# A threshold-attention and MLP kernel: mask operations split around the threshold, rounded weights used a step later, one plain MLP chunk, and no making up of MLP work that had to wait

## The chip, the cores and the metric

The kernel runs on one core of one Trainium2 chip. A core has five engines with a queue each: TensorE (PE in the profile; PEld is its weight loading), VectorE (DVE), ScalarE (ACT), GpSimd (POOL) and SyncE (SP), which here only issues transfers. PE writes into PSUM banks; the other engines move and change data in SBUF and PSUM. Each queue is worked off in order, and an instruction waits until what it reads is written and what it overwrites has been read. The metric is the time of one execution in microseconds (us), and the median of several executions is compared.

## The reference

Eight batches of eight heads, 576 positions, head width 64. Attention keeps only the scores that come within `tau` of the row's maximum; the result, 4608 tokens of 512 values, goes through an MLP with squared ReLU. All is in float32.

```python
scores = scale * np.matmul(q, k.transpose(0, 1, 3, 2))
thresh = np.max(scores, axis=-1, keepdims=True) - tau
scores = np.where(scores >= thresh, scores, -1000000000.0)
scores = scores - np.max(scores, axis=-1, keepdims=True)
attn = np.exp(scores)
attn = attn / (np.sum(attn, axis=-1, keepdims=True) + 1e-09)
out = np.matmul(attn, v)
x = out.transpose(0, 2, 1, 3).reshape(4608, 512)
r = np.maximum(x @ w_in, 0.0)          # w_in 512 x 2048
return (r * r) @ w_out                 # w_out 2048 x 512
```

The MLP weights are handed to the kernel as 64-bit words, and the kernel rounds them to float32 itself, in 32 pieces of 128 x 512.

## The kernel before

All engines' queues stand in the order in which the program text issues (a manual schedule). The main loop (lines 578 to 652) goes over 164 *steps*. A step is one block of 128 queries of a pair of heads (a *visit*), or a last block of 2 x 64 queries with index i = 4, which has one score tile instead of two. The first four pairs are visited twice: steps 0 to 7 take their blocks 0 and 1, steps 8 to 19 their blocks 2 to 4 in visits of three steps; from step 20 on a visit has five steps. Each step issues, roughly in this order:

- `scores` (L200): PE multiplies queries and keys into the PSUM tiles s0 and s1, and DVE takes the maximum of each (L205). There is one pair of score tiles, so the scores of a step wait until the threshold of the step before has read its tiles.
- up to step 36, `turn` for the block of two steps ago: PE transposes (L258, L264, L270), and ACT copies into `wT` (L259 and others). From step 36 on, blocks of later visits are instead turned on DVE (L289) and put in place by 16 transfers each (L300, SP).
- `exponents` (ACT, L213 to L216), then `threshold` (DVE, L228 twice; it masks and sums, then L230 and L231 make the reciprocal), later `divide` (POOL, L238 and L240 twice).
- `mix` (L319): PE multiplies the transposed weights with V, and ACT copies into the ring `xT`.
- at the end of a visit, `prep` (L179): DVE transposes the next visit's queries and keys; `qmid` is copied on POOL (L183).

In steps 2 to 34 a step also rounds a weight piece (or two), `round_weights`, in stages: ACT converts the two halves (L134, L135); DVE makes masks (L137, L138, L140); POOL multiplies (L142); POOL adds the parts into the resident weights (L144), at the end of the step. The raw piece, and a third buffer for attention weights, lie in an area `spare`, which is later the home of quarter sums of the output weights (FT1, FT2, FT4). Where the visit goes on, the masks come between the maximum and the threshold; in a visit's last step they come behind the threshold.

The MLP works on 18 chunks of 256 tokens. A chunk is cut into *pieces* of PE work: 16 `mlp_in` pieces (L368), then either 16 plain `mlp_out` pieces (L399, 512 columns a pass) or 14 `product` pieces (L431). The products are a seven-product form of the second matrix product, on halves of the tokens, the inner dimension and the columns; it needs sums of quarters of the output weights (`sum_quarters`, L390, 16 DVE operations) and sums of halves of the activations (`square_half` on POOL, L357 and L358, and some in `product`'s follow-up on DVE). `PLAIN = 2` chunks are plain.

`fill` is called four times in a step, each time with a quarter of the step's `rate`, in us of PE work; it takes pieces from the queue `waiting` while `left` is at least half a piece (PIECE_US is 1.76), and only if the weights they need are rounded. A piece that has to wait leaves its time in `left`, and later fills make up for it. The rate spreads chunk 0 evenly up to step 35; after that it spreads what is there up to the next steps at which chunks become ready. A piece's follow-up (squares, sums, stores) is issued behind the matmuls of the piece after it (`after`).

Of the kernel before, what the change touches and what calls it, by code (L numbers as in the profile page):

```python
# [19 lines left out]
def kernel(  # L20
# [103 lines left out]
    def round_weights(i, stage):  # L124

        words = weight_area(i).bitcast(U32).rearrange("p (n w) -> p n w", w=2)
        lo, hi = words[:, :, 0], words[:, :, 1]  # L130
        t, e, d = (turned[:, (i % 3 * 3 + x) * WP:(i % 3 * 3 + x + 1) * WP] for x in range(3))
        tu, eu = t.bitcast(U32), e.bitcast(U32)
        if stage == 0:
            nc.scalar.activation(out=e, in_=hi.bitcast(FP32), func=AF.Copy, scale=2.0 ** -112)  # L134
            nc.scalar.activation(out=d, in_=lo, func=AF.Copy, scale=2.0 ** -52)  # L135
        elif stage == 1:
            nc.vector.tensor_scalar(out=tu, in0=hi, scalar1=0x80000000, scalar2=None, op0=ALU.bitwise_and)  # L137
            nc.vector.scalar_tensor_tensor(out=tu, in0=eu, scalar=3, in1=tu, op0=ALU.logical_shift_left,  # L138
                                           op1=ALU.bitwise_or)
            nc.vector.tensor_scalar(out=eu, in0=tu, scalar1=0xFF800000, scalar2=None, op0=ALU.bitwise_and)  # L140
        elif stage == 2:
            nc.gpsimd.tensor_tensor(out=d, in0=d, in1=e, op=ALU.mult)  # L142
        else:
            nc.gpsimd.tensor_tensor(out=weight_piece(i)[1], in0=t.rearrange("p (h d) -> p h d", h=2),  # L144
                                    in1=d.rearrange("p (h d) -> p h d", h=2), op=ALU.add)
# [214 lines left out]
    def mlp_in(j, x):  # L360

        f, at = FORDER[x], j * TCH % RING
        pair = x // 2
        if x % 2 == 0:
            used["h"] = take("mm", (6, 7)) if j < PLAIN else bank[ring3[pair % 3]]
        h = used["h"].rearrange("p (f n) -> p f n", f=2)
        for c in range(NMC):
            nc.tensor.matmul(h[:, x % 2, :], w_in_sb[:, c, f * P:(f + 1) * P], xT[:, c, at:at + TCH],  # L368
                             start=(c == 0), stop=(c == NMC - 1))
        if x == NFT - 1:  # L370
            read_to["x"] = (j + 1) * TCH
        posts = []
        if j == PLAIN:
            posts.append(lambda: sum_quarters(x))
        if x % 2:
            def square():
                to = g[:, f - 1:f + 1, :]
                nc.scalar.activation(out=to, in_=h, func=AF.Relu)  # L378
                nc.gpsimd.tensor_tensor(out=to, in0=to, in1=to, op=ALU.mult)  # L379
                if j >= PLAIN and x % 8 == 7:  # L380
                    square_half(x // 8 * (HF // 2))
            posts.append(square)
        return posts

    def sum_quarters(x):

        which, part = divmod(x, 4)
        f = slice(part * 2, part * 2 + 2)
        to, a, b = ((FT1, Q01, Q00), (FT2, Q11, FT1), (FT4, FT2, Q10), (FT3, Q11, Q01))[which]
        nc.vector.tensor_tensor(out=wo[:, to, f, :], in0=wo[:, a, f, :], in1=wo[:, b, f, :], op=ALU.subtract)  # L390

    def mlp_out(j, f):

# [24 lines left out]
    def product(j, x, half):  # L418
# [4 lines left out]
            ring3[:] = [b, a, c]  # L423
        a, b, c = (bank[y][:, 0:HD] for y in used["abc"])
        p = PRODUCTS[x]
        g0, g1 = g[:, 0:HF, :], g[:, HF:, :]
        left, slot, to = {
            "1": (g0[:, :, 0:P], Q00, a), "5": (gsum[0], FT1, c), "6": (gsum[1], FT2, b), "2": (g1[:, :, 0:P], Q10, a),
# [37 lines left out]
    visits += [(g_, list(range(NBLK + 1))) for g_ in range(HP, NPAIR)]  # L466
    steps = [(n, i) for n in range(len(visits)) for i in visits[n][1]]
    NST = len(steps)
    PLAIN = 2

    def by_dma(n):

# [26 lines left out]
            j += 1  # L499
    PIECE_US = 1.76  # L500
    waiting = deque()
    state = {"us": 0.0, "left": 0.0, "step": 0, "rounded": 0, "then": [], "last": []}

    def early():
        return state["step"] < min(chunk_at)
# [34 lines left out]

    def fill(us):
        state["left"] += us
        while waiting and state["left"] >= PIECE_US / 2 and waiting[0][0] <= state["rounded"]:
            _, fn, *what = waiting.popleft()
            state["left"] -= PIECE_US
            if fn is mlp_out or what[0] <= PLAIN and what[1] == 0:
                after()
            then = fn(*what)
            after()
            state["then"] = then  # L550


    pieces, left = [], n_pieces
# [9 lines left out]
    assert out_from <= first_dma  # L563

    def end_rounding(p):
        round_weights(p, 3)
        state["rounded"] += 1
        if p + RAW < n_pieces:
            load_weights(p + RAW)
# [5 lines left out]
        load_weights(i)  # L575
    prep(0)
    done = 0
    for s in range(END + 1):
        state["step"] = s
        on = s < NST  # L580
        now = []
        if on:
# [45 lines left out]
        if on:  # L628
# [13 lines left out]
        if on:  # L642
            if now:
                end_rounding(now[0])
            for p in now[1:]:
                for stage in range(3):
# [41 lines left out]
```

## Time and profile before

| | us |
|---|---|
| median of 6 runs | 1433.19 (1431.03 to 1433.81) |
| the profiled execution | 1431.03 |
| its span | 1429.2 |
| PE busy in the span | 1379.0 |
| DVE busy | 853.4 |
| POOL busy | 706.6 |
| ACT busy | 435.6 |

The page of a profile shows, for the span of one execution, the busy time of each engine, the busy share in 40 equal slices (a digit is tenths), the chain of work that ended last, and the costliest groups of instructions. Other views of the same trace give busy times by stage (start and end in us from the span's start; then each engine's busy time with its number of instructions, PE's granted clock as a share of full speed, the transfers' share and GB/s), the waits (who waited, for whom, us in all, how often, the longest), and the instructions in order of time (start, duration, engine, line, operation, and in brackets the idle time before it and who ended it). A line such as L140 is a line of the kernel's text. A 256-column float32 pass takes 0.216 us where PE is full, so a piece of eight passes takes 1.73 us.

The steps named in the text start, by the first score matmul (L200), at: 8 at 56.39, 11 at 72.14, 17 at 108.63, 20 at 126.94, 21 at 132.73, 22 at 143.54, 25 at 162.5, 30 at 195.86, 35 at 231.83, 36 at 246.19, 37 at 256.47, 38 at 263.75, 39 at 270.2, 40 at 278.25.

### The profile page before, as it was taken

Reading aid. Unit: us, or ns where it says so; the run is one execution under the profiler, and the core shown is the slowest. Engines: PE = TensorE matmul, PEld = TensorE weight load, DVE = VectorE, ACT = ScalarE, POOL = GpSimd, SP = SyncE. Lnnn points to the kernel's source line nnn. Section 1 sums busy time; section 2 is a strip of 40 time slices with the busy share of each in tenths; the row PEclk is TensorE's granted clock in tenths of the full one; section 3 lists DMA queues with packets and bytes.
Section 4 is the critical chain, followed back from the end, with each engine's and each line's share of the span. In section 5 each row is a group of like instructions: output and inputs, shape, how many; then the busy total and the mean of one; then the engine's idle time right before and its main releaser. Section 6 shows DMA issues by size and latency. Waiting matters only on the chain.

```text
span 1429.2 us, 21996 instructions
## 1 busy us (share of the span) xinstructions
PE 1379.0 (96%) x7412; PEld 1052.9 (74%) x7412; DVE 853.4 (60%) x1770; ACT 435.6 (30%) x1064; POOL 706.6 (49%) x928
## 2 busy tenths in 40 slices
PE   5899988999999999999999999999999999999998
PEld 3676555747777777777777777778777777788887
DVE  5898885557756566666665656566656665621011
ACT  3766664323222313232222232322222232210100
POOL 3688775436454645454545445445445354531321
PEclk9999999999999999999999999999999999999999
DMA  7564441444554555454545554544555445430000
GB/s 150 126 139 122 114 114 40 75 90 84 96 93 91 100 104 101 78 101 89 100 84 103 96 96 89 103 89 92 90 105 94 92 84 108 75 72 15 1 15 15
DMA packets 503823, 125.93 MB, mean 88 GB/s; under 512 B 494912, under 2 KB 495712, under 8 KB 503712
## 3 DMA queue, kind: packets, MB, share of 16 engines
q1 hardware_dynamic: 494448, 107.42, 40.9%
q0 software_dynamic: 6880, 16.82, 3.7%
q8 instruction: 60, 0.98, 0.3%
q10 hardware_dynamic: 2384, 0.30, 0.1%
q14 instruction: 51, 0.42, 0.1%
HBM read 48.63 MB, written 9.44 MB: 41 GB/s over the span
## 4 chain that ended last, share of the span: by engine, by line
PE 83%; DVE 7%; SPq 3%; issue 3%; POOL 2%; ACT 1%; DMA 1%; DVEq 0%; POOLq 0%; ACTq 0%
PE bank L368 34%; PE bank L431 22%; PE s L200 12%; PE bank L319 10%; PE bank L399 3%; SPq L300 2%; DVE st L205 1%; DVE w L228 1%; DVE turned L138 1%; PE bank L258 1%; DVE turned L289 1%; DVE turned L137 1%; DVE turned L140 1%; DVE wo L228 0%; ACT wT L259 0%
## 5 line engine op out<-in xcount | busy, mean ns | idle before, releaser
L368 PE MATMUL bank<-xT,w_in_sb 128*128 128x256 f32 x2304 | 520.6, 383 | 1.8 <-ACT osb L406 1.2
L368 PEld LDWEIGHTS bank<-xT,w_in_sb 128*128 128x128 f32 x2304 | 432.6, 190 | 82.3 <-issue 21.3
L205 DVE TENSOR_REDUCE st<-s 128x1 f32<-128x576 f32 x288 | 206.9, 753 | 319.0 <-PE s L200 318.7
L228 DVE SCALAR_TENSOR_TENSOR w<-s,st,w 128x576 f32<-128x576 f32 x269 | 207.6, 805 | 71.7 <-ACT w L216 71.6
L240 POOL TENSOR_SCALAR w<-w,st 128x576 f32<-128x576 f32 x269 | 235.6, 883 | 28.8 <-DVE st L231 22.3
L431 PE MATMUL bank<-wo,gsum 128*128 128x256 f32 x1024 | 234.0, 381 | 1.4 <-DVE u_sum L446 1.4
L379 POOL TENSOR_TENSOR g<-g 128x512 f32<-128x512 f32 x144 | 149.3, 1038 | 155.1 <-ACT g L378 131.3
L431 PEld LDWEIGHTS bank<-wo,gsum 128*128 128x128 f32 x1024 | 192.7, 190 | 36.3 <-issue 7.2
L200 PE MATMUL s<-kT,qT 64*128 64x288 f32 x1024 | 175.3, 438 | 27.2 <-DVE w L228 10.0
L238 POOL TENSOR_SCALAR st<-st 128x2 f32<-128x2 f32 (+1 forms) x160 | 37.8, 236 | 324.4 <-DVE w L228 310.9
L216 ACT ACTIVATE w<-s,st 128x576 f32<-128x576 f32 x269 | 184.8, 733 | 0.2 <-ACT st L214 0.2
L319 PE MATMUL bank<-wT,vs 128*64 128x128 f32 (+3 forms) x1700 | 177.7, 357 | 3.8 <-ACT wT L259 3.4
L431 PE MATMUL bank<-wo,g 128*128 128x256 f32 x768 | 178.8, 383 | 2.1 <-DVE osb L450 2.1
L431 PEld LDWEIGHTS bank<-wo,g 128*128 128x128 f32 x768 | 143.8, 190 | 31.5 <-issue 8.2
L200 PEld LDWEIGHTS s<-kT,qT 64*128 64x128 f32 x1024 | 98.8, 190 | 91.0 <-issue 66.5
L289 DVE STREAM_TRANSPOSE turned<-w 128x576 f32<-128x576 f32 x225 | 162.1, 754 | 3.5 <-POOL w L240 3.5
L319 PEld LDWEIGHTS bank<-wT,vs 128*64 128x64 f32 x1700 | 104.7, 140 | 73.9 <-issue 23.2
L378 ACT ACTIVATE g<-bank 128x512 f32<-128x512 f32 x144 | 86.2, 599 | 200.8 <-PE bank L368 200.8
L213 ACT ACTIVATE st<-st 128x2 f32<-128x2 f32 (+1 forms) x160 | 33.3, 208 | 324.7 <-DVE st L205 323.9
L333 ACT COPY xT<-bank 128x256 f32<-128x256 f32 x42 | 15.6, 372 | 279.8 <-PE bank L319 279.8
L444 DVE TENSOR_TENSOR gsum<-g 128x512 f32<-128x512 f32 x32 | 20.8, 681 | 107.3 <-PE bank L431 107.3
L399 PE MATMUL bank<-wo,g 128*128 128x512 f32 x128 | 60.1, 604 | 7.3 <-POOL wo L144 7.0
(69 smaller groups left out, 944.5 us busy)
## 6 DMA issues: line engine op xcount, KB each, us to landing
wT<-turned SPq DMA_DIRECT2D x800, 72.0 KB, 2.2
ql<-in_q_dram SPq DMA_DIRECT2D x126, 72.0 KB, 2.4
wo<-in_moe_w_in_dram SPq DMA_DIRECT2D x16, 512.0 KB, 4.7
wo<-in_moe_w_out_dram SPq DMA_DIRECT2D x16, 512.0 KB, 3.5
out_dram<-osb POOLq DMA_DIRECT2D x32, 256.0 KB, 2.7
vs<-in_v_dram POOLq DMA_DIRECT2D x50, 128.0 KB, 3.4
kl<-in_k_dram SPq DMA_DIRECT2D x63, 72.0 KB, 2.4
kl<-in_k_dram SPq DMA_DIRECT2D x63, 64.0 KB, 2.2
```

What stands on the lines that cost most here:

```text
L200: nc.tensor.matmul(sc[u][:, half, 0:HALF], lhsT, kT[rows, half * HALF:(half + 1) * HALF], start=True, stop=True)
L205: nc.vector.tensor_reduce(out=mx[:, u:u + 1], in_=sc[u][:, :, 0:HALF], axis=AX.XY, op=ALU.max)
L216: nc.scalar.activation(out=w[:, u, :].rearrange("p (h k) -> p h k", h=2), in_=sc[u][:, :, 0:HALF], func=AF.Exp, bias=bias[:, u:u + 1], sca ...
L228: nc.vector.scalar_tensor_tensor(out=wu, in0=sc[u][:, :, 0:HALF], scalar=thr[:, u:u + 1], in1=wu, op0=ALU.is_ge, op1=ALU.mult, accum_out=s ...
L240: nc.gpsimd.tensor_scalar(out=w[:, u, :], in0=w[:, u, :], scalar1=z[:, u:u + 1], scalar2=rcp[:, u:u + 1], op0=ALU.add, op1=ALU.mult)
L289: nc.vector.transpose(wb[:, u * KB:(u + 1) * KB, i % 2, :], w[:, u, :].rearrange("p (k q) -> p k q", q=32))
L319: nc.tensor.matmul(ps[u * D:(u + 1) * D, 0:nq], vs[n % 2][:, u * (NBLK + 1) + c, :], wT[:, cw, cols], start=(c == 0), stop=(c == NBLK))
L368: nc.tensor.matmul(h[:, x % 2, :], w_in_sb[:, c, f * P:(f + 1) * P], xT[:, c, at:at + TCH], start=(c == 0), stop=(c == NMC - 1))
L378: nc.scalar.activation(out=to, in_=h, func=AF.Relu)
L379: nc.gpsimd.tensor_tensor(out=to, in0=to, in1=to, op=ALU.mult)
L399: nc.tensor.matmul(o[t].rearrange("p (h d) -> p h d", h=2), g[:, f, t * P:(t + 1) * P], mov, start=(f == 0), stop=(f == NFT - 1))
L431: nc.tensor.matmul(to, left[:, f, :], wo[:, slot, f, :], start=(f == 0), stop=(f == HF - 1))
```

## The change

Four things change. `round_weights` gets one stage more: the third mask and POOL's multiply become stages 2 and 3, and are issued behind the threshold in every rounding step. A piece may use only weights that were rounded by the end of the step before last (`usable`), not those of the step before. `fill` cuts what is left over at one piece. `PLAIN` becomes 1, so that chunk 1 goes through the products; the quarter sums are issued by `some_sums`, two behind each piece of chunk 1 from step 37 on, and what is left of them ahead of the first products.

```diff
-            nc.vector.tensor_scalar(out=eu, in0=tu, scalar1=0xFF800000, ...)     # stage 1
-        elif stage == 2:
+        elif stage == 2:
+            nc.vector.tensor_scalar(out=eu, in0=tu, scalar1=0xFF800000, ...)
+        elif stage == 3:
             nc.gpsimd.tensor_tensor(out=d, in0=d, in1=e, op=ALU.mult)
...
-        if j == PLAIN:
-            posts.append(lambda: sum_quarters(x))
+        if j == PLAIN and state["step"] > first_dma + 1:
+            posts.append(lambda: some_sums(2))
...
+    sums = [(to, a, b, part) for to, a, b in ((FT1, Q01, Q00), (FT2, Q11, FT1), (FT4, FT2, Q10), (FT3, Q11, Q01))
+            for part in range(4)]
+    def some_sums(count):
+        for to, a, b, part in sums[:count]:
+            f = slice(part * 2, part * 2 + 2)
+            nc.vector.tensor_tensor(out=wo[:, to, f, :], in0=wo[:, a, f, :], in1=wo[:, b, f, :], op=ALU.subtract)
+        del sums[:count]
...
+        if sums:                                   # in product
+            some_sums(16 if x > 1 else 8)
...
-    PLAIN = 2
+    PLAIN = 1
...
-        while waiting and state["left"] >= PIECE_US / 2 and waiting[0][0] <= state["rounded"]:
+        while waiting and state["left"] >= PIECE_US / 2 and waiting[0][0] <= state["usable"]:
...
+        state["left"] = min(state["left"], PIECE_US)
...
+    rounded_by = [0]
     for s in range(END + 1):
         state["step"] = s
+        state["usable"] = rounded_by[-1]
+        rounded_by.append(state["rounded"])
...
             elif now:
                 round_weights(now[0], 1)
-                round_weights(now[0], 2)
...
             if lay and now:
                 round_weights(now[0], 1)
+            if now:
                 round_weights(now[0], 2)
+                round_weights(now[0], 3)
```

More of the change, by code (lines that the diff above doesn't have):

```diff
@@ L383, in mlp_in @@
         return posts
[L385 to L390, printed above, removed]
+    sums = [(to, a, b, part) for to, a, b in ((FT1, Q01, Q00), (FT2, Q11, FT1), (FT4, FT2, Q10), (FT3, Q11, Q01))
[5 more added lines that the diff above has]
+        del sums[:count]
     def mlp_out(j, f):
@@ L425, in product @@
         p = PRODUCTS[x]
+        if sums:
+            assert state["step"] > first_dma + 1
+            some_sums(16 if x > 1 else 8)
         g0, g1 = g[:, 0:HF, :], g[:, HF:, :]
@@ L501 @@
     waiting = deque()
-    state = {"us": 0.0, "left": 0.0, "step": 0, "rounded": 0, "then": [], "last": []}
+    state = {"us": 0.0, "left": 0.0, "step": 0, "rounded": 0, "usable": 0, "then": [], "last": []}
     def early():
@@ L565, in end_rounding @@
     def end_rounding(p):
-        round_weights(p, 3)
+        round_weights(p, 4)
         state["rounded"] += 1
@@ L645 @@
             for p in now[1:]:
-                for stage in range(3):
+                for stage in range(4):
                     round_weights(p, stage)
```

## The prediction

> **What bounds the kernel now.** I read the page first (busy shares, then the slices), then the stages between the starts of certain steps, then the waits of PE in the worst stage, then the timeline around them. The page:
>
> ```profile
> PE 1379.0 (96%) x7412; PEld 1052.9 (74%) x7412; DVE 853.4 (60%) x1770; ACT 435.6 (30%) x1064; POOL 706.6 (49%) x928
> ...
> PE   5899988999999999999999999999999999999998
> ...
> DVE  5898885557756566666665656566656665621011
> ...
> POOL 3688775436454645454545445445445354531321
> PEclk9999999999999999999999999999999999999999
> ```
>
> The reader is to see two regimes: from the seventh slice on PE is full and DVE and POOL are half idle; before it DVE and POOL are nearly as busy as PE. The same by stages (start, length, then busy PE, PEld, DVE, ACT, POOL):
>
> ```profile
> 72.14:126.94 54.80, 52.41 (x427) 40.42 (x427) 50.70 (x99) 38.30 (x95) 47.33 (x53) 1.00 0.52 125
> 126.94:162.50 35.56, 32.80 (x230) 22.35 (x229) 30.34 (x59) 21.49 (x53) 26.96 (x32) 0.95 0.40 106
> 162.50:195.86 33.36, 30.19 (x210) 18.49 (x209) 29.12 (x56) 22.00 (x54) 24.32 (x28) 0.95 0.43 115
> 195.86:231.83 35.97, 29.88 (x209) 17.56 (x208) 30.49 (x58) 19.01 (x48) 24.91 (x29) 1.00 0.39 91
> 231.83:246.19 14.36, 12.68 (x74) 9.27 (x73) 3.56 (x8) 5.42 (x12) 8.99 (x13) 1.00 0.31 82
> ...
> 360.00:1260.00 900.00, 895.66 (x4626) 691.69 (x4627) 563.40 (x1192) 241.27 (x603) 438.00 (x608) 1.00 0.51 94
> ```
>
> Steps 11 to 19, 20 to 24, 25 to 29, 30 to 34 and step 35 are the first five. From step 35 on PE is the bound, so PE work taken out there is time saved, and PE work moved there costs its length. In steps 11 to 34 nothing is full, and PE waits for others:
>
> ```profile
> PE bank L399 <- POOL wo L144: 7.0, 5, 2.6
> PE s L200 <- DVE w L228: 4.9, 5, 1.7
> PE s L200 <- DVE wo L228: 3.4, 3, 2.1
> ```
>
> **The change part by part.** Each part is set against the profiled execution, 1431.0 us (span 1429.2 and 1.8 around it), which is 2.2 below the median of 1433.2.
>
> (a) *One plain chunk.* Chunk 1's second half goes from 64 passes of 512 columns to 112 of 256. The chain of waits prices both:
>
> ```profile
> 305.91 5.35 PE bank L399 x12
> ...
> 313.98 1.07 ACT osb L406 x2
> ...
> 1348.21 24.17 PE bank L431 x112
> ```
>
> 5.35 / 12 is 0.446, times 64 is 28.5; the new form is 24.2. PE is full there: -4.4 (a four-pass stretch at 1.73 makes it -3.5 at least). Around it: 4 more POOL additions of 1.28, 11 more DVE operations of 0.41 to 0.73, and one more store of 0.6 on POOL's queue, spread over steps 37 to 44, in which POOL and DVE are half idle (DVE's share is in (e)): 0. The osb wait (1.07 of ACT) stays: the chunk after the plain one opens on bank 6, as chunk 2 does now, and bank 6 is copied out last. SP's queue issues the same loads in the same order.
>
> (b) *Rounded weights used a step later.* PE's waits for L144 go: 7.0 on L399 and 0.6 on L368. Not all of it was on the path: after the 2.56 wait at 197.9 the next scores were only 1.2 late against the threshold that frees their bank, after the 1.35 wait 1.25 late; the 1.69 in step 35, the 1.14, the 0.6 and the 0.2 count whole. 6.1 of 7.6: -6.1. Bounds -7.6 (all) and -2 (the last two steps alone, where PE is the late one). What is late next is the threshold, (c).
>
> (c) *The third mask (L140) and POOL's multiply (L142) go behind the threshold,* in all rounding steps but the last of a visit, whose order stays. L140 stood between the reduction and the threshold, 0.43 alone:
>
> ```profile
> 75.81 1.30 POOL L240 TENSOR_SCALAR wo<-wo,st 128x576 f32<-128x576 f32 x1
> ...
> 76.45 0.94 DVE L140 TENSOR_SCALAR turned<-turned 128x512 uint32<-128x512 uint32 x1
> ...
> 220.41 1.26 POOL L144 TENSOR_TENSOR wo<-turned 128x512 f32<-128x512 f32 x1
> ...
> 220.50 1.46 DVE L137 TENSOR_SCALAR turned<-wo 128x512 uint32<-128x512 uint32 x1
> ```
>
> The masks stretch until the POOL instruction beside them has ended: L137 from 0.42 to 1.46, L140 to 0.94 and 1.38. The exponentials take 1.1 from the end of the reduction (235.63 less 234.52, a step without masks), so two masks (1.11 and 0.1 between) cover it, and the third only delays. Where PE then waited for the threshold (0.8, 1.65, 0.32, 1.71, 2.12, 0.39 from step 9 on) I take out L140's time in that step, never more than the wait: 0.43, 0.43, 0.32, 0.94, 1.38, 0.39, together -3.9. What now waits behind L140: on DVE the next reduction, which idles 0.24 to 0.54 for its scores today, so 0.43 just fits; on POOL the multiply, and behind it the divide (L238, L240) and L144, all some 1.7 later. The divide is read by the transposes two steps on and L144 by the MLP two steps on, so that is covered by one step (5 to 7 us). Bounds over the 20 steps so changed: a threshold 0.45 earlier in each, -9; and +7, if L140 meets a whole POOL instruction before each reduction (0.81 more in 20 steps is 16) against the 9. I take -3.9, from the waits themselves.
>
> The Trainium skill (SBUF — State Buffer, Who interferes with whom) says that whichever of the two engines starts first keeps the shared ports for its whole instruction and the other blocks fully. That speaks against this part: POOL is busy right behind the threshold, where L140 now stands, and half an L240 or L144 before each of 20 of them would be an estimated +10. The rows agree on the blocking, but L140's mean in these stages is 0.61 against 0.43, so the sum is -9.9 by the row and about 0 by the rule; I go by the row.
>
> (d) *Work that had to wait is not made up for.* Followed through the filling rule, step 17 loses its piece (back in 19), steps 20 and 21 have none, 22 has three, and at the end of step 35 five pieces more are still to come. Those five cost 5 x 1.73 later and free as much in steps 20 to 35: 0. Step 35, now 14.36, is PE 5.4 with one piece: its 1.69 wait is in (b). The loss is in dry steps, bounded by the threshold chain:
>
> ```profile
> 130.47 0.55 PE L258 MATMUL bank<-ident,w 128*128 128x128 f32 x3
> 132.73 1.78 PE L200 MATMUL s<-kT,qT 64*128 64x288 f32 x7 [1.71 <-DVE w L228]
> ...
> 135.35 4.83 PE L368 MATMUL bank<-xT,w_in_sb 128*128 128x256 f32 x16
> ```
>
> Today's only dry step, 20, lasts 5.8. Steps 17 to 19 become 5.8 + 7.1 + 6.4 (scores 1.17, transposes 1.21, mixing 1.24, pieces 1.73 each) = 19.3 for 18.3. Steps 20 to 22 become 5.8 + 5.8 + 8.3 and 1.3 for a slow clock after the dry steps (16 passes took 4.76, elsewhere 3.46), 21.2, against 21.8 less one piece, 20.1. Together +2.1. Bounds 0 and +7 (the slow clock in both dry steps and the next too: scores 1.94 for 1.17, mixing 2.2 for 1.24).
>
> The Trainium skill (TensorE: Matmul & The Clock Gate, What's actually happening) puts the slow clock behind an idle window of some 3.4 us. The row shows it behind 1.71 of idle, with 0.95 granted in that stage; by the rule the 1.3 would fall away.
>
> (e) *The 16 quarter sums, two per piece in steps 37 to 39.* They are 0.65 to 0.80 each, formerly one per piece. From the start of scores in step 37: reduction to 2.7, L289 to 4.1, threshold and reciprocals to 6.2, six sums to 10.5 (PE's step ends at 9.0); step 38 likewise to 16.6, four sums to 19.5; step 39: reduction, L289, two sums, threshold to 24.2, then qT and kT (1.45) to 25.7, where PE wants them at 23.3. That is +2.4, at the place that is already tight:
>
> ```profile
> 360.17 1.24 PE L200 MATMUL s<-kT,qT 64*128 64x288 f32 x8 [0.40 <-DVE kT L179]
> ```
>
> Bounds 0 (POOL out of the way, 0.65 each) and +4.
>
> Sum: -4.4 - 6.1 - 3.9 + 2.1 + 2.4 = -9.9, so 1421.1 for the profiled execution, 1423.3 for the median; I say 1423.5.
>
> **The rivals.** *The DVE and POOL cycle is what binds steps 8 to 34.* For: between 195.86 and 231.83 POOL's 24.9 and the masks and small operations beside it fill the stage. If the new order lets them overlap better, (c) is -12 (0.6 in each of 20 steps; the walk from 216.66 to 223.13, 6.47, would shorten to 5.9): -18.0, median 1415. Against: PE's own work in steps 11 to 19 leaves only 2.4 of 54.8.
>
> *Slower: L140 behind the threshold holds the next reduction.* Place: between L231 and L205 in 20 steps; price: a POOL instruction of 0.81 to 1.28 ahead of it each time. With (c) at +11.5 (0.58 net in each) the sum is +5.5, median 1438.7. It decides from +6.0, 0.3 net in each step. For: L230 in that very place is stretched from 0.17 to 0.89 today. Against: POOL there is mostly running L142, which now comes later.
>
> *The gain is eaten by dry steps and sums:* (d) +7, (e) +4, (b) -3: -0.3, no change, 1432.9. For: 0.95 clock already. *The rounding change does nothing for the end,* only (a): excluded as a whole, since the L144 waits of step 35 are on PE's path.
>
> **How the numbers follow.** Forecast (1418 to 1429) 0.48; better overlap, around 1415, 0.23; eaten, around 1433, 0.13; slower, around 1439, 0.16. The range leaves out a few hundredths of the second below 1411 and most of the fourth above 1435. Measurement can tell 0.2% (2.9 us). Faster takes the first two and 0.06 of the third, 0.77; the same 0.07; slower 0.16.
>
> **What would show it.** Right: no PE wait for L144; L399 at half its count and L431 at 1904; shorter waits of L200 for L228 in steps 9 to 33; step 35 near 5.5 us; PE idle and a lower clock around step 20; a wait of L200 for kT of 1 to 3 us near step 40. Wrong: L140's mean above 0.8, a larger idle of L205, POOL waiting longer for L140 than its 26.3 us now, or the stretch from step 20 to 34 no shorter than 105 us.

## The result and the profile after

The changed kernel takes 1430.14 us (median of 22 executions, 1425.60 to 1433.44), the kernel before 1433.35 (45 executions, 1430.17 to 1436.11): a ratio of 0.997 with a 95% interval of 0.9962 to 0.9978. That is faster by 3.2 us in the medians and 4.3 by the ratio, where 9.9 was forecast; the median lies 1.1 above the stated range of 1418 to 1429. The profiled executions differ by 4.74 (1426.29 against 1431.03). The changed kernel's executions lie in two groups, near 1426.3 and near 1430.7; the profiled one is of the lower.

In the page of the changed kernel PE is as full as before, with 3.8 us less work, and POOL has 15 us more:

```profile
PE 1375.2 (97%) x7460; PEld 1064.1 (75%) x7460; DVE 861.8 (60%) x1781; ACT 435.0 (31%) x1063; POOL 722.0 (51%) x933
...
PE   5898989999999999999999999999999999999998
...
DVE  5999886875657566657565656565656665621011
...
POOL 3688876645454545454545445545445444531321
PEclk9999999999999999999999999999999999999999
```

The stages between the same steps as before (20 to 24, 25 to 29, 30 to 34, step 35, and a long stretch behind; start and end, length, busy PE, PEld, DVE, ACT, POOL, then the clock granted to PE; the last two numbers are the transfers' share and GB/s):

```profile
127.64:158.25 30.61, 27.73 (x221) 19.85 (x220) 27.39 (x55) 21.39 (x53) 26.62 (x28) 1.00 0.44 115
158.25:193.63 35.38, 32.76 (x214) 20.31 (x213) 30.57 (x58) 19.87 (x49) 27.17 (x30) 0.90 0.45 116
193.63:228.71 35.08, 31.33 (x210) 19.23 (x209) 28.95 (x57) 21.40 (x51) 27.04 (x29) 0.90 0.38 90
228.71:234.12 5.41, 5.41 (x42) 3.35 (x41) 4.24 (x8) 3.27 (x8) 4.64 (x7) 1.00 0.54 87
360.00:1260.00 900.00, 897.61 (x4639) 695.14 (x4639) 565.16 (x1195) 240.73 (x601) 439.63 (x608) 1.00 0.51 94
```

Step 35 is short, as foreseen. Steps 20 to 24 lost 4.95 (35.56 before), but hold two pieces fewer, so 1.5 net; steps 25 to 29 became 2.0 longer (33.36 before), of which 1.73 is one piece more that now stands there; steps 30 to 34, with as many pieces as before, lost only 0.9 (35.97). Steps 25 to 34 now run at a clock of 0.90. The waits of PE in steps 11 to 35 (72 to 235 us; who waited for whom, us in all, how often, the longest) tell why:

```profile
PE s L201 <- DVE w L229: 8.3, 5, 3.8
PE s L201 <- DVE wo L229: 2.3, 1, 2.3
```

In the same window of the kernel before:

```profile
PE bank L399 <- POOL wo L144: 5.3, 4, 2.6
...
PE s L200 <- DVE wo L228: 2.6, 2, 2.1
PE s L200 <- DVE w L228: 2.4, 3, 1.7
...
PE bank L368 <- POOL w_in_sb L144: 0.6, 1, 0.6
```

So 5.9 us of waits for the addition L144 stood beside 5.0 us of waits for the threshold. The first are gone, with the 1.69 in step 35; the second have grown to 10.6.

By place, with a moved piece counted at the forecast's 1.73 us:

| stretch | before | after | pieces fewer | net |
|---|---|---|---|---|
| up to step 8 | 56.39 | 55.46 | 0 | -0.9 |
| steps 8 to 19 | 70.55 | 72.18 | 0 | +1.6 |
| steps 20 to 34 | 104.89 | 101.07 | 1 | -2.1 |
| step 35 | 14.36 | 5.41 | 4 | -2.0 |
| from step 36 to the end | | | 5 more | -1.3 |

Ahead of step 36 that is -3.4 where (b), (c) and (d) were to bring -7.9. Behind it, it is -1.3 where (a) and (e) were to bring -2.0. In detail both halves of this second sum were larger than forecast. PE's groups show the new form and that its small waits behind DVE (2.1 and 1.4 before) are gone:

```profile
L438 PE MATMUL bank<-wo,gsum 128*128 128x256 f32 x1088 | 249.3, 382 | 0.0
L438 PE MATMUL bank<-wo,g 128*128 128x256 f32 x816 | 188.3, 381 | 0.0
...
L403 PE MATMUL bank<-wo,g 128*128 128x512 f32 x64 | 32.3, 626 | 0.2 <-ACT g L379 0.2
```

And the timeline of PE at step 40 (start, us, what; in brackets the idle time before and who ended it) shows the wait for the keys, with the slow scores and mixing behind it:

```profile
273.79 2.29 PE L201 MATMUL s<-kT,qT 64*128 64x288 f32 x8 [3.45 <-DVE kT L180]
276.01 2.84 PE L320 MATMUL bank<-wT,vs 128*64 128x256 f32 x20
```

### The profile page after: what moved, and what is told of

Its sections match the earlier page's. It is cut to its first block, busy times and chain, and to the rows that moved or that the text cites. A ratio compares the mean times of both kernels' runs of the same rounds, so it can differ in the third digit from the quotient of the medians.

```text
span 1424.5 us, 22123 instructions
## 1 busy us (share of the span) xinstructions
PE 1375.2 (97%) x7460; PEld 1064.1 (75%) x7460; DVE 861.8 (60%) x1781; ACT 435.0 (31%) x1063; POOL 722.0 (51%) x933
## 4 chain that ended last, share of the span: by engine, by line
PE 86%; DVE 6%; issue 2%; ACT 2%; SPq 1%; DMA 1%; POOL 1%; DVEq 0%; POOLq 0%; ACTq 0%
PE bank L369 35%; PE bank L438 25%; PE s L201 13%; PE bank L320 10%; PE bank L259 1%; PE bank L403 1%; DVE w L229 1%; DVE turned L138 1%; DVE st L206 1%; ACT wT L260 1%; DVE turned L290 1%; SPq L301 1%; DVE wo L393 1%; DVE turned L137 0%; ACT w L217 0%
## 5 line engine op out<-in xcount | busy, mean ns | idle before, releaser
L206 DVE TENSOR_REDUCE st<-s 128x1 f32<-128x576 f32 x288 | 207.0, 753 | 302.9 <-PE s L201 302.9
L241 POOL TENSOR_SCALAR w<-w,st 128x576 f32<-128x576 f32 x269 | 239.3, 897 | 27.1 <-DVE st L232 19.1
L438 PE MATMUL bank<-wo,gsum 128*128 128x256 f32 x1088 | 249.3, 382 | 0.0
L438 PEld LDWEIGHTS bank<-wo,gsum 128*128 128x128 f32 x1088 | 204.4, 190 | 38.4 <-issue 10.0
L201 PE MATMUL s<-kT,qT 64*128 64x288 f32 x1024 | 178.7, 444 | 38.9 <-DVE w L229 16.9
L438 PE MATMUL bank<-wo,g 128*128 128x256 f32 x816 | 188.3, 381 | 0.0
L438 PEld LDWEIGHTS bank<-wo,g 128*128 128x128 f32 x816 | 153.6, 190 | 27.8 <-issue 5.3
L379 ACT ACTIVATE g<-bank 128x512 f32<-128x512 f32 x144 | 86.1, 598 | 205.8 <-PE bank L369 205.7
L184 POOL COPY qmid<-qT 64x64 f32<-64x64 f32 x64 | 18.9, 295 | 101.5 <-DVE qT L180 99.6
```

The costliest lines, as they stand in the source:

```text
L201: nc.tensor.matmul(sc[u][:, half, 0:HALF], lhsT, kT[rows, half * HALF:(half + 1) * HALF], start=True, stop=True)
L206: nc.vector.tensor_reduce(out=mx[:, u:u + 1], in_=sc[u][:, :, 0:HALF], axis=AX.XY, op=ALU.max)
L241: nc.gpsimd.tensor_scalar(out=w[:, u, :], in0=w[:, u, :], scalar1=z[:, u:u + 1], scalar2=rcp[:, u:u + 1], op0=ALU.add, op1=ALU.mult)
L438: nc.tensor.matmul(to, left[:, f, :], wo[:, slot, f, :], start=(f == 0), stop=(f == HF - 1))
```

## The experiments

Every kernel is compared with executions of the kernel before on the same chip; those had medians of 1433.1 to 1434.2 (1431.45 in the single execution beside `again1` and `again2`). Diffs are against the changed kernel unless said otherwise.

**What the sums cost.** `one_sum` issues one quarter sum per piece and one ahead of each product.

```diff
-            posts.append(lambda: some_sums(2))
+            posts.append(lambda: some_sums(1))
...
-            some_sums(16 if x > 1 else 8)
+            some_sums(1)
```

> The changed kernel, but one quarter sum behind each piece of chunk 1 from step 37 on, instead of two, and one ahead of each product until none is left. The theory from the changed trace: the sums cost 5.0 us there (step 39 at 11.5 us with a wait of 3.45 us for kT, step 40 at 10.4 us with a slow clock, against 8.05 and 8.8 before), because each sum and POOL's square sums block each other. Spread out, step 39 falls to 8 to 9 us and the whole is 3 to 5 us faster than the changed kernel, about 1426 us. The rival: DVE and POOL have no room in steps 37 to 43 whatever the spacing, so the wait only moves to the end of the next visit (step 44): within 1.5 us of the changed kernel.

Measured: 1423.87 us (1421.32 to 1425.59), ratio 0.9933 (0.9921 to 0.9946). From step 36 to step 45 it takes 75.5 us, the changed kernel 80.4. So (e) cost 4.9, by the medians 6.3, and not 2.4. DVE of the changed kernel in steps 38 and 39:

```profile
262.86 2.94 DVE L393 TENSOR_TENSOR wo<-wo 128x512 f32<-128x512 f32 x4
265.73 0.74 DVE L206 TENSOR_REDUCE st<-s 128x1 f32<-128x576 f32 x1
266.39 1.42 DVE L290 STREAM_TRANSPOSE turned<-w 128x576 f32<-128x576 f32 x2
267.74 3.33 DVE L393 TENSOR_TENSOR wo<-wo 128x512 f32<-128x512 f32 x2
270.99 0.81 DVE L229 SCALAR_TENSOR_TENSOR w<-s,st,w 128x576 f32<-128x576 f32 x1
```

and POOL beside it:

```profile
267.58 1.27 POOL L358 TENSOR_TENSOR gsum<-g 128x512 f32<-128x512 f32 x1
268.92 1.60 POOL L359 TENSOR_TENSOR gsum<-gsum,g 128x512 f32<-128x512 f32 x1
270.49 1.48 POOL L380 TENSOR_TENSOR g<-g 128x512 f32<-128x512 f32 x1
```

Two sums, which take 0.65 to 0.69 where POOL is idle, take 3.33 together: each ends 0.55 behind the POOL operation beside it (L358, then L359). The threshold and the keys' transpose stand behind them.

`warm39` asks what the clock adds: six extra matmuls ahead of the scores of step 40, never read, where PE would stand idle.

```diff
+        if s == 40:
+            for c in range(6):
+                nc.tensor.matmul(bank[4][:, 0:TCH], w_in_sb[:, c % NMC, 0:P], xT[:, c % NMC, 0:TCH],
+                                 start=(c == 0), stop=(c == 5))
```

> The changed kernel with six extra matmuls (2.6 us, into bank 4, never read) ahead of the scores of step 40, where PE otherwise stands 3.45 us in front of the transposed keys. If the sums cost 3.45 us of wait and 1.5 to 3 us more because the clock is slow behind that wait, step 39 stays at about 11.5 us, the scores of step 40 take 1.24 instead of 2.29 and step 40 takes 8.9 instead of 10.4 to 11.8: 1427 to 1428.5 against 1430. If the slow scores have another cause (their operands, DVE or POOL at work beside them), step 40 stays above 10 and the time at 1430 or above.

Measured: 1428.07 us (1424.88 to 1432.94), ratio 0.9966 (0.9954 to 0.9977); the interval overlaps that of the changed kernel, so the timing alone doesn't settle it. The profile does:

```profile
273.90 1.24 PE L201 MATMUL s<-kT,qT 64*128 64x288 f32 x8 [0.86 <-DVE kT L180]
275.07 2.38 PE L320 MATMUL bank<-wT,vs 128*64 128x256 f32 x20
```

Step 39 is unchanged (11.49), step 40 falls from 10.37 to 8.86. So (e) is 3.45 of wait and 1.5 of a slow clock behind it.

**The rounding changes apart.** `no_split` puts the third mask and the multiply back ahead of the threshold: (c) undone.

```diff
             elif now:
                 round_weights(now[0], 1)
+                round_weights(now[0], 2)
+                round_weights(now[0], 3)
...
-            if now:
                 round_weights(now[0], 2)
-                round_weights(now[0], 3)
```

> The changed kernel, but the third mask and POOL's multiply go back between the reduction and the threshold; all else as changed. The prediction's theory (c): the split gains 3.9 us, so this is some 4 us slower than the changed kernel, about 1434 us, and the waits of PE scores for the threshold grow in steps 9 to 33. The rival, from the trace of the changed kernel: the split loses, because POOL's multiply, divide and addition all come 1.7 us later and the masks of the steps with two weight pieces (24 and 29) then stand behind them; step 25 to 26 and 30 to 31 there lost 2.3 and 3.8 us in waits for the threshold, and a slow clock follows. Then this is 3 to 6 us faster than the changed kernel, about 1425 us, with steps 24 to 31 (60.5 us in the changed kernel) at 54 to 57 us.

Measured: 1433.52 us, ratio 1.0005 (0.9994 to 1.0016); `delay_only`, the same undone in `one_sum`:

> One sum per piece, rounded weights used a step later, the third mask and the multiply in their old places: (b) and (d) without (c). If the parts add up as the other runs say, 1427.2 us (1433.5 of the changed kernel with the old order, less 6.3 for the sums), so that (b) with its dry steps is worth 3.2 and (c) 3.4. If (b) and (c) only work as a pair: 1430 to 1432, no better than products_only, and (c) on top of it is worth 6 to 8.

Measured: 1427.87 us, ratio 0.9965 (0.9952 to 0.9978), 4.0 above `one_sum`. So (c) is worth 3.4 in the one pair and 4.0 in the other (4.6 to 5.0 by the ratios): the size of the forecast's 3.9. These two kernels show something else: with (b) and (d) and without (c), step 36 starts at 239.93 and 238.44 instead of 246.19, but the five pieces fewer explain 8.65 of that. Net, (b) and (d) alone were worth +2.4 and +0.9 in these profiled executions (that of `delay_only` is the fastest of its seven, 2.4 below its median), not -4.0.

`use_at_once` takes the step's delay away and leaves the rest. Chunk 1 then starts in step 35, and a transposition overwrites a bank that one of its pairs has half filled, so part of chunk 1 is not the reference's; the work is the same.

```diff
-        state["usable"] = rounded_by[-1]
-        rounded_by.append(state["rounded"])
+        state["usable"] = state["rounded"]
```

> The changed kernel, but a piece may again use the weights rounded in the step before. The prediction's theory (b): the waits of PE for POOL's addition come back, 6 us, less 2 us for the dry steps that go: some 4 us slower than the changed kernel, about 1434 us. First rival: the additions are later now than before the change, so the waits are larger than the 7.6 us of before: 6 to 9 us slower. Second rival: what binds steps 20 to 34 is DVE with POOL, and PE's waits for POOL fill time in which it would have waited for the threshold anyway: within 1.5 us of the changed kernel, although 5 to 8 us of waits for the addition are seen.

Measured: 1441.29 us, ratio 1.0057, 11 above the changed kernel. `products_only` and `no_lag` repeat this cleanly, with one sum per piece and chunk 1 kept out of step 35; they differ from each other only in (c).

```diff
             # both: use_at_once, one_sum, and in fill
+            if waiting[0][2] >= PLAIN and state["step"] <= first_dma:
+                break
             # products_only: also no_split
```

> The kernel before with part (a) alone: one plain chunk, the quarter sums one per piece and one ahead of each product, chunk 1 kept out of step 35; masks in the old order, rounded weights used at once. If (a) is worth the -4.4 of its count of passes: 1428.8 us against 1433.2 for before, with the waits for the addition of the rounding still there (about 7 us). If the rounding changes are worth less than forecast and (a) more: 1424 to 1426. If (a) is eaten by its sums and stores: 1432 or more.

> As products_only, but with the third mask and the multiply behind the threshold, (c) alone on top of (a). If (c) is independent of when weights are used, it gains the 3.4 us that it gains in the changed kernel: about 3.4 below products_only, 1425.4. If (c) needs the step's delay, because behind the threshold the multiply and the addition come 1.7 us later and PE stands in front of the addition: 3 to 8 us above products_only, 1432 to 1437, with the wait of L399's successor for L145 above 10 us in sum.

Measured: `products_only` 1430.42, ratio 0.9977 (0.9968 to 0.9986); `no_lag` 1442.57, ratio 1.0064 (1.005 to 1.0078). The first does not price (a): keeping chunk 1 out of step 35 brought a 3.87 us wait for the copying of `osb` into step 36, and slow pieces behind it. But the pair is clean: without the step's delay, (c) costs 12 us, with it, it gains 4. PE's waits in `no_lag` from 72 to 235 us (steps 11 to 33 and the start of 34; a wait of 3.35 for L145 follows at its end):

```profile
PE bank L403 <- POOL wo L145: 8.7, 6, 2.6
PE bank L369 <- POOL w_in_sb L145: 3.2, 1, 3.2
PE s L201 <- DVE w L229: 2.6, 2, 1.5
```

The multiply behind the threshold makes the addition late, and PE stands in front of it. (b) is what lets (c) pay.

`no_cap` lets work that had to wait be made up for.

```diff
-        state["left"] = min(state["left"], PIECE_US)
```

> The changed kernel without the cap on what fill carries over: 12 pieces then stand in step 36 (4 now), 3 instead of 2 in step 18 and 4 instead of 3 in step 22. If the cap only moves PE work from one full step to another (the prediction's zero for moved work), this is within 1.5 us of the changed kernel. If the burst starves DVE, ACT and POOL of new scores for the 21 us of step 36 and they are late afterwards, it is 2 to 5 us slower; if the denser step 36 lets the quarter sums and transposes of step 39 run while PE is busy, it is 2 to 4 us faster.

Measured: 1439.25 us, ratio 1.0041, 9 above the changed kernel and outside what was expected. Step 36 issues 12 pieces in 26.90 us, and the sums then come in a burst ahead of the products (step 39: 15.61 us, 4.1 of it a wait for L358). This burst is a second change, so the run does not price the missing cut of `left` alone.

**Dry steps and the clock.** `warm` puts four extra matmuls, never read, into steps 17, 20 and 21, which have no piece.

```diff
+        if s in (17, 20, 21):
+            free = bank[(6, 7)[(used["mm"] + 1) % 2]]
+            for c in range(NMC):
+                nc.tensor.matmul(free[:, 0:TCH], w_in_sb[:, c, 0:P], xT[:, c, 0:TCH], start=(c == 0), stop=(c == NMC - 1))
         fill(quarter)
```

> The changed kernel with four extra matmuls (1.73 us, into the free bank that the next piece takes, never read) in the steps that lost their piece, 17, 20 and 21. If the dry steps cost what they cost through the slow clock behind them (step 18 takes 7.4 us in one profiled execution and 10.6 in another with the same instructions), the extra work takes the place of an idle PE, all executions fall together near 1426 us, median 1426 to 1427 against 1430, and step 18 takes 6.5 to 7.4. If the clock has nothing to do with the dry steps, the executions stay spread from 1426 to 1431 and the median at 1430. If the extra work lies on the path: 1432 to 1435.

Measured: 1428.09 us, five executions from 1427.14 to 1429.80, ratio 0.9963 (0.9949 to 0.9976): closer together than the changed kernel's and without its upper group, but with its interval overlapping. It fits neither theory exactly. In its profile step 18 took 7.38, as expected, but step 40 took 11.80 where the changed kernel's took 10.37: behind the wait for the keys the clock was slow for 6.83 us, and for 3.41 in the changed kernel. What the clock can do shows in two kernels that issue the same instructions up to step 36. PE in step 18 of the changed kernel:

```profile
113.88 1.70 PE L201 MATMUL s<-kT,qT 64*128 64x288 f32 x7 [1.92 <-DVE w L229]
...
115.99 1.99 PE L369 MATMUL bank<-xT,w_in_sb 128*128 128x256 f32 x8
```

and in `one_sum`:

```profile
114.01 2.51 PE L201 MATMUL s<-kT,qT 64*128 64x288 f32 x7 [1.93 <-DVE w L229]
...
117.36 3.78 PE L369 MATMUL bank<-xT,w_in_sb 128*128 128x256 f32 x8
```

After the same wait the step took 7.37 us at a granted clock of 1.00 and 10.56 us at 0.68. The traces show what made the difference: the granted clock changes only at points that lie 3.413 us, or a multiple of it, apart in an execution. Between such points are *windows*; some of them around step 18 in the changed kernel (start and end, length, busy PE and the other engines, clock):

```profile
109.72:113.13 3.41, 1.99 (x25) 1.38 (x23) 3.27 (x7) 2.07 (x6) 3.08 (x5) 1.00 0.39 135
113.13:116.55 3.42, 2.66 (x19) 1.96 (x20) 3.35 (x9) 2.66 (x7) 2.72 (x3) 1.00 0.84 231
```

and in `one_sum`, where the second stretch is two windows:

```profile
111.22:114.63 3.41, 1.48 (x13) 0.75 (x9) 3.28 (x8) 2.67 (x8) 3.22 (x4) 1.00 0.38 111
114.63:121.46 6.83, 6.81 (x27) 4.91 (x28) 5.98 (x12) 3.50 (x9) 5.95 (x7) 0.50 0.52 156
```

In `one_sum` the whole wait (112.08 to 114.01) fell into one window, which kept PE busy for only 1.48 us, and the next two windows ran at half clock. In the changed kernel the end of a window divided the same wait (111.96 to 113.88), both windows had more work, and the clock stayed. `again1` and `again2` profile the changed kernel twice more.

> The changed kernel once more, for a second profile. Its executions lie near 1426.3 or near 1430.7 us. If the clock behind an idle PE makes the difference, an execution near 1430.7 has step 18 at 9 to 10.6 us instead of 7.4, or step 40 at 11.5 to 11.8 instead of 10.4, with the same waits ahead of them and a granted clock of 0.83 to 0.9 there, and the same times from step 45 on; an execution near 1426.3 has the step lengths of the profile shown. If the difference lies elsewhere, the steps from 45 on differ.

> As again1: the changed kernel, a third profile. Near 1430.7 us: longer steps 18 to 26 or 40 at a lower granted clock, behind the same waits; near 1426.3: as the profile shown.

Measured: 1426.14 and 1426.56, both at the lower level, with the step lengths of the first profile within 0.1 us. So it is not shown that the two levels of the changed kernel (near 1426.3 and 1430.7) come from this clock. The mean granted clock of the whole execution does not part them either: it is 0.990 to 0.996 up to 1427.1 us and 0.987 to 0.992 from 1430.1 us on, five times 0.991 as in most of the lower group. The cause stays open.

`even` spreads the first 12 pieces over steps 11 to 21 in `one_sum`, and no step is dry; `paced` does so over steps 11 to 20, lets weights of the step before be used from the middle of a step on and keeps chunk 1 out of step 35.

```diff
     def rate(s):
+        if s <= HP * FIRST + HP * 3 + 1:                      # even; paced: without + 1, and + 1 - s below
+            first = sum(x[2] == 0 and x[1] is mlp_in and x[3] < 12 for x in waiting)
+            return PIECE_US * first / (HP * FIRST + HP * 3 + 2 - s)
```

> The kernel with one sum per piece (1423.9 us), and the first 12 pieces of chunk 0 spread evenly over steps 11 to 21, so that none of these steps is without one; weights used a step later throughout. If the dry steps cost time through idle PE and slow clock: 1420 to 1422, steps 17 to 22 in 39 us or less. If the clock is slow for other reasons, or the pieces moved make the steps 22 to 34 longer: 1424 or more.

> The kernel with one sum per piece (1423.9 us), with the pieces spread so that no step from 11 to 35 is without one: the first 12 pieces evenly over steps 11 to 20, and the weights of the step before usable from the middle of a step on (chunk 1 kept out of step 35). If the dry steps and the slow clock cost about 3 us: 1420 to 1421. If PE then waits for the additions again, which the delay of a step had removed: 1424 to 1428, with waits for L145 of 3 us and more.

Measured: `even` 1421.21, ratio 0.9924 (0.991 to 0.9937); steps 17 to 22 take 36.5 us (43.3 in `one_sum`, with one piece more, 1.73, and the slow step 18). Some is lost in step 25, where PE waits 4.9 for a square (L379). `paced` 1431.31, ratio 0.9982: the waits for L145 are back (4.4 us), and the 3.9 for `osb` in step 36, as in `products_only`.

**When the weights come.** In steps 25 and 26, and 30 and 31, the changed kernel spends 17.9 and 19.1 us, where pairs of other steps take 10 to 12. These follow steps 24 and 29, which round two weight pieces. DVE there:

```profile
159.33 0.46 DVE L137 TENSOR_SCALAR turned<-wo 128x512 uint32<-128x512 uint32 x1
159.90 1.58 DVE L138 SCALAR_TENSOR_TENSOR turned<-turned 128x512 uint32<-128x512 uint32 x1
161.51 1.15 DVE L141 TENSOR_SCALAR turned<-turned 128x512 uint32<-128x512 uint32 x1
162.58 1.41 DVE L206 TENSOR_REDUCE st<-s 128x1 f32<-128x576 f32 x2
```

The masks of the second piece, stretched beside POOL, stand ahead of the next step's reduction; its threshold comes late, and PE stands and then runs slowly (at half clock for 6.83 us from 167.75 and from 201.88 on):

```profile
167.74 2.51 PE L201 MATMUL s<-kT,qT 64*128 64x288 f32 x7 [2.28 <-DVE wo L229]
...
202.86 2.51 PE L201 MATMUL s<-kT,qT 64*128 64x288 f32 x7 [3.75 <-DVE w L229]
```

`early_weights` rounds those second pieces in steps 5 and 7 instead, in `one_sum`; `early_after` does it in the changed kernel, `early_before` in the kernel before, `one_early` in `one_sum` for step 24 only, and `one_each` rounds one piece in every step from 2 to 33.

```diff
-            x = int(n > 0 and i == 0)
+            x = int(n > 0 and i == 0 or n > 1)       # one_early: n > 2; one_each: int(n > 0)
         else:
-            x = 2 if n >= 2 * HP and i == NBLK else 1
+            x = 1                                     # one_early: 2 if s == 29 else 1
```

> The kernel with one sum per piece, in which steps 5 and 7 round a piece each and steps 24 and 29 one instead of two; weights are then early enough that no step from 11 to 34 is without a piece. If the second piece of steps 24 and 29 makes the steps behind them long (25, 26, 30 and 31 take 9.5, 5.9 to 8.4, 9.2 and 9.1 to 9.9 where others take 5 to 6) and the dry steps cost as said: steps 17 to 34 fall from 118 to 108 to 112, steps 5 to 8 grow by 1 to 3: 1416 to 1421. If the long steps have another cause, or the loads of the early pieces hold up the first steps: 1424 to 1428.

> One sum per piece; only step 7 rounds a piece more, and step 24 one instead of two; step 29 keeps two. If the second piece of a step makes the two steps behind it long, steps 25 and 26 fall from 15.4 to 18 together to 11 to 12, and steps 30 and 31 stay at 18 to 19: 1417 to 1419. If the length of these steps comes from the pieces of the MLP that come late, all four become shorter or none.

> The kernel before with its weights rounded earlier (a piece each in steps 5 and 7, one instead of two in 24 and 29), nothing else. If the second pieces of steps 24 and 29 cost what they do in any order, and nearly all of the 11.6 us that this brought to the changed kernel with one sum per piece comes from them and from the additions coming in time: 1422 to 1425 against 1433.5. If the gain is one of the change alone (dry steps that the delay makes, masks behind the threshold), the kernel before gains little: 1430 to 1434.

> The changed kernel with its weights rounded earlier, sums two per piece as in the change. If the sums and the early weights are independent, 1412.3 plus the 5.0 to 6.3 of the sums: 1417 to 1419. If the sums cost less where the first steps end earlier: 1413 to 1415.

> One sum per piece and one weight piece in every step from 2 to 33, so that the rounding ends one step earlier; chunk 1 is kept out of step 35, and the last rows of chunk 0 are copied out at the end of that step. If the weights are what the steps up to 36 wait for: 1409 to 1411.5. If a piece more in step 3 holds up the first steps, or step 36 waits longer for the bank that is copied out (1.6 us in the changed kernel, 3.9 where chunk 1 was kept out of step 35): 1413 to 1416.

| kernel | median us | ratio (95%) |
|---|---|---|
| `early_weights` | 1412.29 | 0.9857 (0.9844 to 0.9871) |
| `one_early` | 1419.30 | 0.9899 (0.9886 to 0.9913) |
| `early_before` | 1425.30 | 0.9946 (0.9933 to 0.9960) |
| `early_after` | 1417.78 | 0.9893 (0.9879 to 0.9906) |
| `one_each` | 1412.58 | 0.9854 (0.984 to 0.9867) |

`one_early` tells the cause: steps 25 and 26 fall from 15.4 in `one_sum` to 11.5, and the 2.31 wait for the threshold in them is gone (the other 1.73 is a piece that moved to an earlier step). Steps 30 and 31, still behind two weight pieces, take 20.3 (18.3 in `one_sum`), with the wait and the slow scores:

```profile
200.52 2.51 PE L201 MATMUL s<-kT,qT 64*128 64x288 f32 x7 [4.52 <-DVE w L229]
```

Its gain in time is not all from this wait: `one_early` also has pieces in steps 17 and 21, two of the dry steps. But with the same 18 pieces in them, steps 20 to 34 of `early_after` take 89.9 us instead of 101.1. The cost is one of the kernel before too (-8.1 there, 7.7 by the ratio); the change makes it dearer (-12.4 in the changed kernel, 11.0 by the ratio). In `early_after` the threshold waits in steps 11 to 35 shrink from 10.6 to 2.1:

```profile
PE s L201 <- DVE w L229: 1.2, 4, 0.6
PE s L201 <- DVE wo L229: 0.9, 2, 0.5
```

With the weights early, the change is worth 7.5 us (1425.30 to 1417.78) instead of 3.2. Step 36 starts at 225.15 in `early_after` and 241.94 in `early_before`; less the 8.65 of the five pieces, that is -8.1. So (b), (c) and (d) together bring the -7.9 that was forecast for them once the weights are early; how it is shared among them is not shown there. `one_each` shortens step 36 from 12.8 to 10.8 and loses it again in the first steps (step 11 starts 1.2 later) and in step 41 (7.7 for 6.5); it and `early_weights` are the fastest, 21 us below the kernel before.

## Why the prediction was right or wrong

The direction was right, but of the 9.9 us forecast only 3.2 came by the medians (4.7 between the profiles), and 1430.14 lies above the stated 1418 to 1429. The step that failed is in (b): the waits for the addition were counted as 6.1 us gained, and "what is late next is the threshold, (c)" was taken to be paid for by (c). The runs show the waits for the threshold growing by 5.6 us in its place, so that (b) and (d) together cost 0.9 to 2.4 us instead of gaining 4.0. Second, (e) was mis-sized, 4.9 for 2.4. That (a) brought more than forecast hid part of both, and this was luck.

Of the signs that the prediction named, the missing waits for the addition, the counts (64 and 1904 passes) and step 35 (5.41) came as said; the waits for the threshold grew where they were to shrink, the wait for the keys was 3.45 instead of 1 to 3, and the lower clock around step 20 did not come in this profile (1.00 in steps 20 to 24). Of the signs of being wrong one came: POOL waited 32.6 us for L141, 26.3 before for L140. That is in the first steps (17.3 for 7.5 up to 72 us); from 72 to 235 us it waited less, 15.4 for 18.8.

Two readings in the prediction were loose. PE is full from the eighth slice on, not the seventh (its digit is 8). And "in steps 11 to 34 nothing is full" does not hold for steps 11 to 19, where its own row has PE busy for 52.41 of 54.80 us. Neither is a term of the sum.

- **(a)**, forecast -4.4. The stretch from step 36 on is -1.3 net; without the 4.9 of the sums it is -6.2. (Behind step 45 the kernel before took 1110.5 us in its own profile and 1109.1 in that of `early_before`, with the same instructions, so about 1.3 of this is within what executions differ by.) The passes are as priced (24.17 us for 112 in the chain of waits after as before). The step "the osb wait stays" failed: the wait of 1.07 went, one of 1.57 came in step 36, and 3.5 us of waits for `osb` and `u_sum` behind the products went, against one new wait of 1.65 for the keys. That (a) is larger for this reason is argued from the two traces; no run shows it alone.
- **(b)**, forecast -6.1. The waits for the addition went, all 7.6 of them. The failing step is "what is late next is the threshold, (c)": it was late by more than what (c) took off. In steps 11 to 35 its waits doubled, from 5.0 to 10.6; 6.0 of that is behind the two steps that round two pieces, which the prediction had only named as steps "whose order stays". Step 30 shows it: before, PE waited 2.56 for the addition, and the next scores were counted as 1.2 late. After, PE is there earlier, but DVE still has the masks of the second piece: the reduction starts 4.4 us after the step's first scores (2.6 before), the threshold 8.3 (7.9 before, with the third mask still ahead of it), and PE waits 3.75 for it. (b) and (d) together came out at +2.4 and +0.9 instead of -4.0 (`no_split`, `delay_only`), the largest miss.
- **(c)**, forecast -3.9: right in size, 3.4 to 4.0 in two pairs. The rival in which the mask holds the next reduction falls: L141's mean over 72 to 235 us is 0.57 (0.63 before), and the idle time ahead of L206 fell from 14.6 to 13.0. But the cover, "covered by one step", is (b) itself; without (b) the same edit costs 12.
- **(d)**, forecast +2.1, bounds 0 to +7. The dry steps came where the filling rule put them. Steps 17 to 22, less a piece's 1.73, are 0.2 longer than before in the changed kernel's profile, without a slow clock, and 4.9 longer in that of `one_sum`, with it; parts of (b) and (c) are in these numbers. The slow clock came in other places too: 0.90 in steps 25 to 34, behind the threshold waits. `even`, without dry steps, is 2.7 below `one_sum` by the medians (the intervals overlap). The change is worth 4.3 more where the weights come early and no step is dry, but there the second pieces of steps 24 and 29 are gone too. So (d) is not priced by itself.
- **(e)**, forecast +2.4, bounds 0 to +4: measured 4.9. The place was right, the keys of step 40. The walk had two sums ahead of the threshold of step 39 at 0.65 to 0.80 each and they took 3.33, so the wait was 3.45; and the slow clock behind it, which (d) had and (e) had not, added 1.5.

The rival "the gain is eaten by dry steps and sums" was nearest in mechanism: (e) +4, (b) weak, slow clock. It gave 1432.9, its (a) was too small, and its largest term, +7 for dry steps, is not what the profiles show (0.2 and 4.9).

On the two rules that were weighed: for L141 the row was right and the estimated +10 did not come. But the rule of the Trainium skill (SBUF — State Buffer, Who interferes with whom) has a line for the quarter sums that was passed over: a DVE instruction with two SBUF inputs contends with a GpSimd instruction that reads SBUF. The sums have two such inputs, and the 1.67 each beside L358 and L359 agree with it. For the clock, the trace's 1.71 was a better guide than the page's idle window: PE ran at 0.68 behind 1.93 of idle, and the window before was not idle but held 1.48 us of PE work.

## What to carry to other kernels

A wait that is taken out uncovers the next one in the same steps: before counting its whole length, ask which chain would have let PE go on, and look for steps that carry twice the work of that chain. Where PE may stand for 2 us and more, add the slow clock behind the wait to its price (3.2 us in step 18, 1.5 in step 40), and expect it in some executions and not in others. And an edit that delays a producer is only as cheap as the slack of its consumer: here (c) was worth -4 or +12, depending on (b).

## What the runs showed of the hardware

- Behind a wait of the same length PE's clock may be slow or not: 1.92 us of idle was followed by a step at 1.00 (7.37 us) in one execution, 1.93 by the same step at 0.68 (10.56 us) in another. In each of the twenty profiles the granted clock changes only on a grid of 3.413 us, to half clock and back, for 3.41, 6.83 or 10.24 us; how the grid lies to the span's start differs from execution to execution (0.50 us behind it in the changed kernel, 1.99 in `one_sum`). Of the windows at full clock up to 1400 us, all 45 in which PE was busy for less than 1.5 us were followed by one at half clock, 20 of the 129 with 1.5 to 2.4 us, and none with more. The Trainium skill (TensorE: Matmul & The Clock Gate, What's actually happening) has a free-running window of 3.4 us, so that the outcome depends on where in it the work falls; the grid agrees with that.
- Behind the 3.45 us wait of step 40 the clock was slow in each profile of the changed kernel, and with 2.6 us of it filled with matmuls (`warm39`) the clock stayed at 1.00.
- Two DVE subtractions of 0.65 us took 3.33 us beside three POOL operations in a row (1.27, 1.60 and 1.48 us); each ended 0.55 behind one of them.
